# Third group of x transposed by DMA, three groups' scales made at once, GpSimd's work reordered around the second group's gelu scale

## The chip, the cores and the metric

One core of one Trainium2 chip. The metric is the device time of one execution in microseconds (us). The kernel before takes 410.85 us, the median of three runs (410.72 to 411.11).

## What is computed

x has S = 2048 tokens of D = 448 channels, F is 1792.

```
xn = layernorm(x)
A  = irfft2(rfft2(xn) * (w_r + i w_i))
h  = gelu(layernorm(xn) @ w1)                 # [S, D]
hs = concat(shift(h[:, 0:112], +1), shift(h[:, 112:224], -1),
            shift(h[:, 224:336], +2), shift(h[:, 336:448], -2)) @ w2
x1 = xn + hs
h2 = gelu(layernorm(x1) @ w3) @ w4
out = x + A + x1 + h2
```

The shifts run along the tokens and fill with zeros. The change is in the part up to hs; what follows it on TensorE is w3, w4 and the Fourier filter.

## The kernel before

x lies in 16 blocks of 128 tokens, `xb(b)`, each [128, 448], two to a tile `xt`. They are worked on in four groups, GRP = [14, 15, 0, 1], [2, 3, 4, 5], [6, 7, 8, 9], [10, 11, 12, 13], called groups 0 to 3 below (the title's third group is group 2). Every float32 factor of a product is split into a float16 high part and the float16 remainder, and every product is three passes of float16 matmuls into PSUM. A row of 448 channels takes four slices of channels, the last of them 64 wide, which is why a 448 x 448 product of one block has 11 matmuls.

For each group the front part of the kernel does this:

- `norm1(g)`: statistics of each block on VectorE (L306, L307), a start value of 1/sqrt by integer arithmetic (L323 to L326), the negative mean (L328), and then each block is normalised in place with this start value (L333, L336) by the engine that `apply` names. The start value is exact enough for a float16 split once the later scales correct it.
- `refine()`, ten small operations on GpSimd (L345 to L354): the accurate 1/sqrt, and `gsc`, the scale under the first gelu.
- `scales()`, eight small operations on GpSimd (L358 to L365): `cs`, by which the block is scaled where hs is added, and the scale and bias of xn for the filter.
- The block is turned, so that channels lie on the partitions, and split. `T1(g)` with `transpose_split` does this for groups 0 to 2: TensorE transposes (L387, 16 for a group) into a PSUM bank, ScalarE copies the high part out (L391), VectorE subtracts (L401). `turn(3)` does it for group 3: ScalarE copies the high part (L868), VectorE makes the remainder in two pieces (L869, L870), and one DMA transpose per block on SyncE's queue (L871) writes the turned float16 block.
- `w1_unit(g, i)`: 11 matmuls (L427), gelu on ScalarE (L467), the high part on ScalarE (L468), the remainder in two halves on VectorE (L470). The pieces are written into a shifted layout in `x2mem`, and where a block of shifted h is complete, a DMA transpose turns it (L478).
- `w2_tile(b)`: 11 matmuls with the turned h block (L486) and an evacuation on VectorE that needs `cs` (L487).

Weights are scaled by a power of two from their mean square. `powers` makes it: squares on ScalarE (L253), a sum on VectorE (L258), a matmul with ones (L260), five small VectorE operations. `split_w` then splits: for w2 GpSimd scales (L276), ScalarE copies the high part (L277), GpSimd subtracts (L278); two DMAs copy parts of w2p to the other partitions (L933, L934). The last part of w3 and 1344 KB of w4 (`w3raw`, L223, and `w4half`, L238) are loaded behind the last h transpose of group 1.

The first units of group 0 are computed side by side in four PSUM banks, `first`. Units 22 and so on are unit 2 of group 2. A tile scheduler puts the instructions of each engine in one fixed order, and each engine and each DMA queue takes its own in that order. `behind(key)` says that what follows in the block is put after the instructions named; `pins` do that for the statistics of single blocks. SyncE's queue holds loads, h transposes and x transposes together. After the front part come tiles 4 to 7, units of group 3 (30 to 33), and, from the first L407 on, w3.

Of the kernel before, what the change touches and what calls it, by code (L numbers as in the profile page):

```python
# [32 lines left out]
EPS = 1e-5  # L33
# [3 lines left out]
PIN = [("a3",), ("a3",), ("a3",), ("a3",)]  # L37
# [88 lines left out]
def body(tc, nc, x, wf, w1, w2, w3, w4, c_g, c_n, c_small, out):  # L126
# [185 lines left out]
    xn_scale, xn_bias = {}, {}  # L312

    def norm1(g, apply, pins=None):

        bs = GRP[g]
        n, b0 = len(bs), bs[0]
        mv = pc.tile([128, 4, 2], F32, name=f"mva{b0}")
        stats([xb(b) for b in bs], f"a{b0}", mv, pins)
        a = pc.tile([128, 2 * n], F32, name=f"va{b0}")  # L320
        yi = pc.tile([128, 2 * n], I32, name=f"vy{b0}")
        y = yi.bitcast(F32)
        V.tensor_scalar(out=a[:, n:], in0=mv[:, :n, 1], scalar1=1.0 + EPS, scalar2=EPS * EPS, op0=ALU.mult, op1=ALU.add)  # L323
        V.tensor_scalar(out=a[:, 0:n], in0=mv[:, :n, 1], scalar1=EPS, scalar2=None, op0=ALU.add)
        V.tensor_single_scalar(yi, a.bitcast(I32), 1, op=ALU.logical_shift_right)
        V.tensor_scalar(out=yi, in0=yi, scalar1=-1, scalar2=0x5F3759DF, op0=ALU.mult, op1=ALU.add)  # L326
        nm = pc.tile([128, n], F32, name=f"nma{b0}")
        i = V.scalar_tensor_tensor(out=nm, in0=mv[:, :n, 0], scalar=-1.0, in1=y[:, n:], op0=ALU.mult, op1=ALU.mult)  # L328
        after["c", g] = (i.ins,)
        for k, b in enumerate(bs):  # L330
            y_, m_ = y[:, n + k:n + k + 1], nm[:, k:k + 1]
# [3 lines left out]
            else:  # L335
                i = apply[k].tensor_scalar(out=xb(b), in0=xb(b), scalar1=y_, scalar2=m_, op0=ALU.mult, op1=ALU.add)  # L336
                if apply[k] is V:
                    after["n", g] = (i.ins,)

        q, z = (pc.tile([128, 2 * n], F32, tag=f"v{t}", bufs=2, name=f"v{t}{b0}") for t in "qz")  # L340
        w, r = (pc.tile([128, 2 * n], F32, name=f"v{t}{b0}") for t in "wr")
        nm1 = pc.tile([128, n], F32, name=f"nm{b0}")

        def refine():
# [9 lines left out]
            P.tensor_scalar(out=gsc[:, 4 * g:4 * g + 4], in0=r[:, n:], scalar1=r1, scalar2=None, op0=ALU.mult)  # L354

        def scales():
            c, r1st, u = cs[:, 4 * g:4 * g + 4], w[:, 0:n], w[:, n:]
            P.tensor_tensor(out=r1st, in0=r[:, 0:n], in1=y[:, 0:n], op=ALU.mult)  # L358
            P.tensor_tensor(out=u, in0=r[:, n:], in1=r[:, n:], op=ALU.mult)
            P.tensor_tensor(out=c, in0=y[:, n:], in1=a[:, n:], op=ALU.mult)  # L360
            P.tensor_tensor(out=c, in0=c, in1=u, op=ALU.mult)
            P.tensor_tensor(out=c, in0=c, in1=r1st, op=ALU.mult)
            P.tensor_scalar(out=c, in0=c, scalar1=s12[:, 0:1], scalar2=None, op0=ALU.mult)
            P.tensor_tensor(out=nm1, in0=mv[:, :n, 0], in1=r1st, op=ALU.mult)
            P.tensor_scalar(out=nm1, in0=nm1, scalar1=-1.0, scalar2=None, op0=ALU.mult)  # L365
            for k, b in enumerate(bs):
                xn_scale[b], xn_bias[b] = r1st[:, k:k + 1], nm1[:, k:k + 1]
        return refine, scales
# [11 lines left out]
    def transpose_split(srcs, dst, key, ts=range(4), at=0, tags=("tr",) * 4, late=None):  # L380
        c = slice(128 * at, 128 * at + 128 * len(srcs))
        for t in ts:
# [9 lines left out]
            todo.append((key, t, i, lo, pt, dst[:w, t, c]))  # L392
        if late is None:
            low()

    todo = []

    def low():
        while todo:
            key, t, i, lo, pt, hi = todo.pop(0)  # L400
            j = V.tensor_tensor(out=lo, in0=pt, in1=hi, op=ALU.subtract)  # L401
            after[key, t] = after[key] = i.ins, j.ins
# [486 lines left out]
    with behind("e1"):  # L889
        low()  # L890
    for t in range(4):
        if t >= 1:
            with behind("p1"):
                T1(0, [t])
# [220 lines left out]
```

## Time and profile before

| what | us |
|---|---|
| median of three runs | 410.85 |
| profiled execution | 410.88 |
| its span | 409.1 |
| PE busy in the span | 400.4 (98%) |
| DVE, ACT, POOL busy | 336.9, 256.1, 103.2 |

PE, DVE, ACT, POOL and SP are TensorE, VectorE, ScalarE, GpSimd and SyncE. PEld is the weight load of a matmul, SPq the time that SyncE's queue takes to issue a DMA. A timeline row is the start, the duration of the stretch, the engine, the line, the operation, the tile written and the tiles read, the shape, and the count; what stands in brackets is the time that the engine idled just before, and what ended it. A row `xN` in a timeline gives N of them that follow each other. A DMA row in the list of issues is the size and the median time from issue to landing. The granted clock of TensorE is 1.00 at full rate.

### The profile page before, as it was taken

The page shows a single profiled execution, that of the slowest core. Times are in us where ns is not written, and L with a number is a line of the kernel's source. Part 1 is how long each engine was busy: PE and PEld are TensorE (multiplying, and loading weights), DVE is VectorE, ACT ScalarE, POOL GpSimd, SP SyncE. Part 2 cuts the span into 40 slices and gives each one's busy share as a digit, 9 for nine tenths or more (in the row PEclk, how much of TensorE's full clock was granted, in tenths as well). Part 3 has the DMA queues.
Part 4 walks back from the last instruction along what each step waited for, and adds up shares of the span by engine and source line. Part 5 has one row for each costly group of instructions (what it writes and reads, how often), then busy time and mean ns, then how long its engine had stood idle before and what let it go on. Part 6 is the DMA issues. An engine that isn't in the chain of part 4 may idle for free.

```text
span 409.1 us, 8749 instructions
## 1 busy us (share of the span) xinstructions
PE 400.4 (98%) x3391; PEld 297.5 (73%) x3391; DVE 336.9 (82%) x702; ACT 256.1 (63%) x434; POOL 103.2 (25%) x173
## 2 busy tenths in 40 slices
PE   8899999999999999999999999999999999999996
PEld 3455545765667777877787887877777779998995
DVE  5998999999856895998798888956899999965645
ACT  4689699882558866655598878863454445453431
POOL 7787630112145948310022111110000000000000
PEclk9999999999999999999999999999999999999999
DMA  8977995558779652536255666510011023100101
GB/s 275 373 286 139 238 177 140 110 115 178 102 200 292 219 151 77 182 136 179 68 144 143 155 149 164 146 31 13 22 70 69 24 85 96 46 2 2 45 2 45
DMA packets 54596, 52.07 MB, mean 127 GB/s; under 512 B 35678, under 2 KB 48542, under 8 KB 54556
## 3 DMA queue, kind: packets, MB, share of 16 engines
q1 hardware_dynamic: 54556, 51.53, 46.4%
q8 instruction: 26, 0.43, 0.4%
q14 instruction: 14, 0.11, 0.1%
HBM read 38.28 MB, written 3.67 MB: 103 GB/s over the span
## 4 chain that ended last, share of the span: by engine, by line
PE 86%; DVE 5%; DMA 3%; POOL 2%; ACT 1%; SPq 1%; issue 1%
PE pw L407 33%; PE acc L816 23%; PE pw L486 6%; PE side L786 4%; PE acc L786 3%; PE pu L675 3%; PE ps L575 3%; PE pe L696 2%; PE pp L630 2%; PE px L647 2%; PE py L717 2%; PE pw L427 2%; DMA xt<-x 1%; DVE sta L306 1%; DVE xT L401 1%; DMA w2p<-w2p 1%
## 5 line engine op out<-in xcount | busy, mean ns | idle before, releaser
L407 PE MATMUL pw<-x2mem,w3p 128*128 128x256 f16 x1232 | 152.0, 273 | 0.0
L407 PEld LDWEIGHTS <-w3p 128*128 128x128 f16 x1232 | 119.0, 98 | 19.6
L816 PE MATMUL acc<-w4p,hf 128*128 128x448 f16 (+1 forms) x516 | 104.2, 348 | 0.0
L816 PEld LDWEIGHTS <-hf 128*128 128x128 f16 x516 | 50.1, 98 | 37.5
L734 ACT ACTIVATE pw<-pw,pe 128x512 f32<-128x512 f32 x42 | 27.5, 654 | 31.7 <-PE pw L407 31.6
L737 DVE SCALAR_TENSOR_TENSOR hf<-pw,h,hf 128x512 f16<-128x512 f32 x42 | 31.3, 745 | 12.7 <-ACT hf L736 12.4
L486 PE MATMUL pw<-w2p,h 128*128 128x448 f16 x176 | 35.7, 353 | 1.6 <-DMA h<-x2mem 1.2
L427 PE MATMUL pw<-w1p,xT 128*128 128x448 f16 x176 | 34.8, 352 | 0.7 <-ACT w1p L280 0.4
L656 POOL TENSOR_TENSOR z<-te 128x450 f32<-128x450 f32 x16 | 15.7, 981 | 70.7 <-DVE te L654 65.8
L736 ACT ACTIVATE hf<-pw,h 128x512 f16<-128x512 f32 x42 | 28.8, 685 | 5.0 <-PE acc L816 4.0
L486 PEld LDWEIGHTS <-h 128*128 128x128 f16 x176 | 17.1, 98 | 17.2 <-DMA h<-x2mem 1.9
L427 PEld LDWEIGHTS <-xT 128*128 128x128 f16 x176 | 17.2, 98 | 16.6 <-issue 1.1
L752 ACT ACTIVATE hz<-g,h 128x896 f16<-128x896 f32 x14 | 14.6, 1042 | 22.9 <-DVE g L749 22.9
L786 PEld LDWEIGHTS <-hz 128*128 128x128 f16 x294 | 28.2, 98 | 0.6
L637 ACT ACTIVATE pf<-pp 64x450 f16<-64x450 f32 x32 | 17.3, 542 | 12.6 <-DVE pf L638 9.6
L638 DVE TENSOR_TENSOR pf<-pp,pf 64x450 f16<-64x450 f32 x32 | 19.9, 622 | 5.1 <-ACT pf L637 4.8
L753 DVE SCALAR_TENSOR_TENSOR hz<-g,h,hz 128x896 f16<-128x896 f32 x14 | 16.1, 1147 | 6.7 <-ACT hz L752 6.7
L558 POOL TENSOR_TENSOR f<-xr 128x452 f32<-128x452 f32 x16 | 19.7, 1250 | 0.6
L566 DVE TENSOR_TENSOR xh<-f,xh 128x452 f16<-128x452 f32 x16 | 14.3, 916 | 4.9 <-ACT xh L565 4.9
L652 ACT ACTIVATE te<-px 64x450 f32<-64x450 f32 x32 | 17.3, 540 | 1.2 <-PE px L647 0.6
L746 ACT ACTIVATE g<-pw,pe 128x512 f32<-128x512 f32 x14 | 9.6, 683 | 11.4 <-PE pw L407 11.4
L555 POOL TENSOR_TENSOR xr<-xf 128x452 f32<-128x452 f32 x8 | 9.2, 1154 | 24.4 <-issue 17.6
(188 smaller groups left out, 712.5 us busy)
## 6 DMA issues: line engine op xcount, KB each, us to landing
wc<-wf SPq DMA_DIRECT2D x32, 225.0 KB, 3.7
wl<-wf SPq DMA_DIRECT2D x8, 450.0 KB, 4.2
xt<-x SPq DMA_DIRECT2D x8, 448.0 KB, 7.8
xf<-x SPq DMA_DIRECT2D x8, 448.0 KB, 4.9
loads<-x SPq DMA_DIRECT2D x7, 448.0 KB, 3.5
out<-xt SPq DMA_DIRECT2D x13, 224.0 KB, 1.9
w3raw<-w SPq DMA_DIRECT2D x3, 896.0 KB, 11.3
gn<-c_g SPq DMA_DIRECT2D x16, 128.0 KB, 3.1
```

Of the source, the lines that this page charges most:

```text
L407: T.matmul(ps_out, wp[:, wi + t, cols], xT[:, xi + t, tok], start=t == 0 and wi + xi == 0, stop=t == 3 and wi == 4)
L427: T.matmul(pm[:, :D], xTs[g][:, xi + t, 128 * i:128 * i + 128], w1p[:, wi + t], start=t == 0 and p == 0, stop=t == 3 and p == 2)
L486: T.matmul(pm[:, :D], h[:, k], w2p[:, w], start=n == 0, stop=n == 10)
L558: P.tensor_tensor(out=f[:, :, k:k + 2].rearrange("p b s d -> p s b d"), in0=u[:, :, 0], in1=u[:, :, 1], op=op)
L637: A.activation(out=hi, in_=src, func=AF.Copy)
L638: V.tensor_tensor(out=lo, in0=src, in1=hi, op=ALU.subtract)
L652: A.activation(out=e[64 * h:64 * h + 64], in_=px_[64 - 64 * h:128 - 64 * h, :2 * DF], func=AF.Copy)
L734: A.activation(out=pm, in_=pm, func=AF.Gelu_apprx_tanh, scale=r3)
L736: i = A.activation(out=h[:, 0], in_=pm, func=AF.Copy, scale=h3)
L737: j = V.scalar_tensor_tensor(out=h[:, 1], in0=pm, scalar=h3, in1=h[:, 0], op0=ALU.mult, op1=ALU.subtract)
L786: m = T.matmul(to, h[:, hi, 128 * blk:128 * blk + 128], b[wi], start=new and n == 0, stop=n == 2 and (last if blk in (2, 5, 3, 0) else end ...
L816: m = T.matmul(to, h[:, hi, o:o + 128], w4p[0][:, wi, f, r], start=first and f % 2 == 0 and n == 0, stop=end and f % 2 == 1 and n == 2, sk ...
```

## The change

`turn` takes the side of its staging tile and the engines for the remainders, and is called for group 2, `turn(2, 0, (V, V, V, V))`, in place of `T1(2)`. Sixteen TensorE transposes, four copies (L391) and four subtractions (L401) go; four copies (L860), eight subtractions (L862, L863) and four DMA transposes (L864) come.

`scales` is a function of its own, and the tiles that it reads (`mva`, `va`, `vw`, `vr`, `vy`) hold all 16 blocks. It is called once for groups 0 to 2, behind the refinement of group 2, and once for group 3: 16 operations, before 32.

The rest is order: all four slices of group 0 are transposed behind w1's power matmul; units 0 and 1 of group 0 are finished ahead of group 1's transposes, units 2 and 3 behind w2's power matmul, which itself comes behind unit 1; block 0 is normalised on GpSimd and not on ScalarE; w2 is split behind group 1's gelu scale on GpSimd and not behind a normalisation of group 2 on ScalarE; the two memsets of the wrap move behind group 2's gelu scale; pins differ.

```diff
-PIN = [("a3",), ("a3",), ("a3",), ("a3",)]
+PIN = [("b0",), ("b0",), ("b0",), ("b0",)]
...
+            i = P.tensor_scalar(out=gsc[:, c], in0=r[:, 1], scalar1=r1, scalar2=None, op0=ALU.mult)
+            after["g", g] = (i.ins,)
+        return refine
+
+    def scales(g, n):
+
+        o = slice(4 * g, 4 * g + 4 * n)
+        c, r1st, u, y, r = cs[:, o], vw[:, 0, o], vw[:, 1, o], vy[:, :, o], vr[:, :, o]
+        P.tensor_tensor(out=r1st, in0=r[:, 0], in1=y[:, 0], op=ALU.mult)
...
+        P.tensor_scalar(out=c, in0=c, scalar1=s12[:, 0:1], scalar2=None, op0=ALU.mult)
+        P.tensor_tensor(out=nm1[:, o], in0=mva[:, o, 0], in1=r1st, op=ALU.mult)
+        P.tensor_scalar(out=nm1[:, o], in0=nm1[:, o], scalar1=-1.0, scalar2=None, op0=ALU.mult)
...
     def wrap_on():
         move(pairs[1], pairs[0], -1)
-        P.memset(pairs[0][0:1], 0.0)
-        P.memset(pairs[2], 0.0)
...
-    def turn(g):
+    def turn(g, side=1, engines=(V, V, V, V)):
 
         xTs[g] = p1.tile([128, 7, 512], F16, tag="xT", bufs=2, name=f"xT{g}")
-        y = stage(f"x{g}", 8 * D, 1, F16).rearrange("p (i n) -> p i n", i=4)
+        y = stage(f"x{g}", 8 * D, side, F16).rearrange("p (i n) -> p i n", i=4)
         for i, b in enumerate(GRP[g]):
             h, x_ = y[:, i], xb(b)
             u = A.activation(out=h[:, 0:D], in_=x_, func=AF.Copy)
-            V.tensor_tensor(out=h[:, 448:512], in0=x_[:, 384:448], in1=h[:, 384:448], op=ALU.subtract)
-            v = V.tensor_tensor(out=h[:, 512:896], in0=x_[:, 0:384], in1=h[:, 0:384], op=ALU.subtract)
+            e = engines[i]
+            e.tensor_tensor(out=h[:, 448:512], in0=x_[:, 384:448], in1=h[:, 384:448], op=ALU.subtract)
+            v = e.tensor_tensor(out=h[:, 512:896], in0=x_[:, 0:384], in1=h[:, 0:384], op=ALU.subtract)
             d = SY.dma_start_transpose(out=xTs[g][:, :, 128 * i:128 * i + 128], in_=h)
...
-    n1 = [norm1(0, [P, V, A, V])]
-    T1(0, range(1), True)
+    n1 = [norm1(0, [P,V,P,V])]
...
-    n = 1
+    n = 2
     for unit in list(enumerate(first))[:n]:
         w1_in(0, [unit], [2, 3])
...
-    n1.append(norm1(1, [P, V, A, V], [("n", 0), ("r1",), ("a0", 0), ("a0", 1)]))
+    n1.append(norm1(1, [P, V, A, V], [("r1",), ("a0", 0), ("w1", 0), ("w1", 1)]))
...
-    with behind("n", 1):
+    with behind("n", 1), behind("u"):
         s2, r2 = powers(m2, 1, "2", first[0][:, 448:512])
+    with behind("p2"):
+        for unit in list(enumerate(first))[2:]:
+            w1_in(0, [unit], [2, 3])
...
-    with behind("a1"):
-        n1.append(norm1(2, [P, V, A, P]))
+    with contextlib.nullcontext():
+        n1.append(norm1(2, [P, V, A, P], [("n", 1), ("n", 1), ("e2",), ("e2",)]))
...
-    with behind("na", 2):
+    with behind("g", 1):
         for k in range(4):
             r = slice(0, 128 if k < 3 else 64)
-            split_w(w2p[r, k], w2p[r, 7 + k], w2s[r, k], s2[r], P)
+            after["w2", k] = split_w(w2p[r, k], w2p[r, 7 + k], w2s[r, k], s2[r], P)
         SY.dma_start(w2p[64:128, 3:7], w2p[0:64, 0:4])
         SY.dma_start(w2p[0:64, 4:7], w2p[64:128, 0:3])
     for k in range(4):
         w1_unit(1, k)
-    T1(2)
+    turn(2, 0, (V, V, V, V))
     with behind("h", 1, 3):
         load_w3([3])
         load_w4(8, 6)
-    n1[2][0]()
-    for n in n1:
-        n[1]()
+    n1[2]()
+    with behind("g", 2):
+        P.memset(pairs[0][0:1], 0.0)
+        P.memset(pairs[2], 0.0)
+    scales(0, 3)
```

The order on the engines differs in the front part only. SyncE's queue, before: h blocks of group 0 and 1's units (`h_470`), then the loads of `w3raw` and `w4half`, then blocks of the next h tile and of group 3's x.

```order
L933 DMA w2p<-w2p 64x1792
L934 DMA w2p<-w2p 64x1344
L478 DMA_TRANSPOSE h_470<-x2mem 128x7x128 x3
L223 DMA w3raw<-w 64x1792 x2
L238 DMA w4half<-w 128x6x448
L478 DMA_TRANSPOSE h_635<-x2mem 128x7x128
L871 DMA_TRANSPOSE xT_757<-x_758 128x7x128 x2
```

SyncE's queue in the change, from the copies of w2p to the same place (`xT_507` is group 2's x, `xT_709` group 3's):

```order
L925 DMA w2p<-w2p 64x1792
L470 DMA_TRANSPOSE h_454<-x2mem 128x7x128
L864 DMA_TRANSPOSE xT_507<-x_508 128x7x128 x2
L470 DMA_TRANSPOSE h_454<-x2mem 128x7x128 x2
L864 DMA_TRANSPOSE xT_507<-x_508 128x7x128 x2
L470 DMA_TRANSPOSE h_454<-x2mem 128x7x128
L223 DMA w3raw<-w 64x1792 x2
L238 DMA w4half<-w 128x6x448
L864 DMA_TRANSPOSE xT_709<-x_710 128x7x128 x2
L470 DMA_TRANSPOSE h_587<-x2mem 128x7x128
```

Four x transposes now stand among the four h transposes ahead of the loads, the w2p copies stand ahead of the first h transpose, and the first transpose behind the loads is one of group 3's x.

TensorE, before, at the end of group 1's units (`pw_13` is unit 3 of group 1, `pta` a bank of transposed slices, `pw_0` tile 0):

```order
L427 MATMUL pw_13_506<-w1p,xT_324 128x448
L387 MATMUL pta_524<-ident,xt_79 128x128 x2
L387 MATMUL pta_524<-ident,xt_80 128x128 x2
L387 MATMUL pta_530<-ident,xt_79 128x128 x2
L387 MATMUL pta_530<-ident,xt_80 128x128 x2
L387 MATMUL pta_536<-ident,xt_79 128x128 x2
L387 MATMUL pta_536<-ident,xt_80 128x128 x2
L486 LDWEIGHTS h_470
L486 MATMUL pw_0_705<-w2p,h_470 128x448
```

TensorE in the change, where the matmuls of one unit or tile (11 of each, each with its weight load) are shown by one row of each kind:

```order
L420 LDWEIGHTS xT_322
L420 MATMUL pw_13_490<-w1p,xT_322 128x448
...
L478 LDWEIGHTS h_454
L478 MATMUL pw_0_657<-w2p,h_454 128x448
...
L420 MATMUL pw_22_606<-w1p,xT_507 128x448
```

Tile 0 now follows group 1's last unit with nothing between, and unit 22, the first of group 2, follows tile 0.

GpSimd, before, around group 2's normalisation (`vy_412`, `nma_417` and `xt_79`, `xt_80` are group 2's):

```order
L451 MEMSET x2mem 1x1792
L345 TENSOR_TENSOR vq_423<-vy_412 128x8
L360 TENSOR_TENSOR cs<-vy_412,va_411 128x4
L336 TENSOR_SCALAR xt_79<-xt_79,vy_412,nma_417 128x448
L336 TENSOR_SCALAR xt_80<-xt_80,vy_412,nma_417 128x448
L346 TENSOR_TENSOR vq_423<-vq_423,va_411 128x8
L278 TENSOR_TENSOR w2p<-w2s,w2p 128x448
```

GpSimd in the change, at the same place:

```order
L352 TENSOR_SCALAR gsc<-vr,pe_205 128x4
L276 TENSOR_SCALAR w2s<-w2s,pe_355 128x448 x3
L276 TENSOR_SCALAR w2s<-w2s,pe_355 64x448
L278 TENSOR_TENSOR w2p<-w2s,w2p 128x448 x3
L343 TENSOR_TENSOR vq_412<-vy 128x8
L362 TENSOR_TENSOR cs<-vy,va 128x12
L336 TENSOR_SCALAR xt_79<-xt_79,vy,nma 128x448
L336 TENSOR_SCALAR xt_80<-xt_80,vy,nma 128x448
L278 TENSOR_TENSOR w2p<-w2s,w2p 64x448
```

Three of w2's four subtractions now stand ahead of group 2's normalisation, directly behind the scalings; before they stood behind it, and a memset stood ahead.

More of the change, by code (lines that the diff above doesn't have):

```diff
@@ L854, in body, with T1 @@
     flat = lambda t: t.rearrange("p a n -> p (a n)")
-    def T1(g, ts=range(4), late=None):
+    def T1(g, ts=range(4)):
         if g not in xTs:
@@ L959, in body @@
     turn(3)
-    n1[0][0]()
-    n1[0][1]()
+    n1[0]()
+    scales(3, 1)
     ln2([0, 1], [A, P])
```

88 lines of the change are left out of this document (35 added, 53 removed).

## The prediction

> **What bounds the kernel now.** I read the page's chain of work first, then the busy time of each engine in windows, then the timelines of TensorE, SyncE, VectorE and GpSimd over 14 to 80 us. The chain, and the windows (start:end and length, busy us of PE, PEld, DVE, ACT and POOL, granted clock, DMA share, GB/s):
>
> ```profile
> PE 86%; DVE 5%; DMA 3%; POOL 2%; ACT 1%; SPq 1%; issue 1%
> ```
>
> ```profile
> 30.00:40.00 10.00, 9.05 (x55) 5.32 (x54) 8.39 (x20) 9.97 (x18) 8.69 (x22) 1.00 0.69 132
> 50.00:60.00 10.00, 9.21 (x49) 4.55 (x48) 9.71 (x34) 9.97 (x20) 4.33 (x13) 1.00 0.87 168
> 120.00:409.00 289.00, 285.81 (x2720) 230.84 (x2718) 232.40 (x407) 167.07 (x285) 52.75 (x50) 1.00 0.34 99
> ```
>
> TensorE sets the end. It idles under 1 us in 30 to 40 and in 50 to 60, and 3.2 of 289 us from 120 on. The two kernels issue the same instructions in the same order on PE from the first L400 (L407 before) on, so the change is worth as much as it moves that point. Here is what PE does until then (start, us, tile, count, idle before it and who ended it):
>
> ```profile
> 19.34 0.38 PE L260 MATMUL pw<-pt,ones 128*128 128x1 f32 x2 [0.75 <-DVE pt L258]
> 20.18 1.97 PE L387 MATMUL pta<-ident,xt 128*128 128x128 f32 x16 [0.46 <-POOL xt L336]
> 21.98 11.32 PE L427 MATMUL pw<-w1p,xT 128*128 128x448 f16 x59
> 33.15 1.47 PE L387 MATMUL pta<-ident,xt 128*128 128x128 f32 x12
> 35.12 1.31 PE L486 MATMUL pw<-w2p,h 128*128 128x448 f16 x6 [0.51 <-DMA h<-x2mem]
> 36.27 0.60 PE L387 MATMUL pta<-ident,xt 128*64 128x128 f32 x4
> 37.69 0.73 PE L486 MATMUL pw<-w2p,h 128*128 128x448 f16 x3 [0.45 <-DMA w2p<-w2p]
> 55.43 2.24 PE L427 MATMUL pw<-w1p,xT 128*128 128x448 f16 x11
> ```
>
> ```profile
> 70.84 0.60 PE L407 MATMUL pw<-x2mem,w3p 128*128 128x256 f16 x4
> ```
>
> One matmul of 448 columns is paced at 11.32/59, about 0.19 us; the landmark is 70.84. The profiled execution took 410.88 us, 0.03 over the median; its span is 409.1, so 1.8 us lie around it.
>
> **What the change takes from TensorE.** The 16 transposes of the third group cost 1.47 + 0.60 = 2.07 us, and the waits of 0.51 and 0.45 stand among them. The copies of w2p (0.45) are issued earlier and should be in place. At the front, group 1's transposes waited 0.75 + 0.46 us. GpSimd's normalisation ended that wait, and it stood behind small scale operations that now come later:
>
> ```profile
> 19.42 0.71 POOL L336 TENSOR_SCALAR xt<-xt,vy,nma 128x448 f32<-128x448 f32 x1
> ```
>
> It can start about 1 us sooner, at the end of the gelu scale; and unit 1 of group 0 (5 matmuls, 0.95 us) now fills the idle time. I put the transposes at 19.2 instead of 20.18, with unit 1 done ahead of them. Group 1's last matmul then ends near 33.15 − 1.0 − 0.8 = 31.4 (0.8 taken of the 0.95, as the fit is not perfect). That is 1.8 us won. By then PE is through with 1.8 + 2.07 us that the old kernel still had ahead.
>
> **What it waits for next: the first h block.** Tile 0 is now next on PE, with nothing in front of it to fill the time. It needs the first h transpose (here from issue, SPq) and its landing:
>
> ```profile
> 32.09 1.34 SPq L478 DMA_TRANSPOSE h<-x2mem  x1
> 34.80 4.37 SPq L478 DMA_TRANSPOSE h<-x2mem  x3
> 39.23 1.22 SPq L223 DMA_DIRECT2D w3raw<-w  x2
> 40.49 0.59 SPq L238 DMA_DIRECT2D w4half<-w  x1
> 46.16 1.23 SPq L478 DMA_TRANSPOSE h<-x2mem  x1
> ```
>
> It was issued at 32.09, tile 0 began at 35.12: about 3.03 us later. The issue comes from a VectorE chain that the change lengthens in front: w2's power matmul now stands behind unit 1 and group 1's transposes, so its scale, made at 20.3, comes later. These are the scale's last step, the subtractions of transposed slices and the block statistics on VectorE, and the w2 scalings on GpSimd:
>
> ```profile
> 20.21 0.14 DVE L267 TENSOR_SCALAR pe<-pe 128x1 int32<-128x1 int32 x1
> 22.83 1.99 DVE L401 TENSOR_TENSOR xT<-pta,xT 128x512 f16<-128x512 f32 x3
> 24.86 2.21 DVE L306 BATCH_NORM_STATS2 sta<-xt 128x6 f32<-128x448 f32 x4
> ```
>
> ```profile
> 21.28 1.26 POOL L276 TENSOR_SCALAR w2s<-w2s,pe 128x448 f32<-128x448 f32 x2
> ```
>
> Four subtractions of 0.66 us now stand ahead of the scale on VectorE, from about 20.5 (0.8 behind the first transposes): with two statistics and the scale's own five steps between them I estimate it at 24.1. GpSimd's four scalings of 0.63 us follow, to 26.6, then its first three subtractions (L278, 1.0 us each) to 29.8. VectorE, with two more statistics (0.55 each) and unit 0's remainder (0.8) behind the scale, reaches group 2's small operations (L324 to L328) at the same moment, about 26.6. What such company does is in these rows:
>
> ```profile
> 16.79 1.03 DVE L325 TENSOR_SCALAR vy<-va 128x8 int32<-128x8 int32 x1
> 28.09 1.01 DVE L323 TENSOR_SCALAR va<-mva 128x4 f32<-128x4 f32 x1
> 29.35 0.17 DVE L326 TENSOR_SCALAR vy<-vy 128x8 int32<-128x8 int32 x1
> 29.76 0.51 DVE L336 TENSOR_SCALAR xt<-xt,vy,nma 128x448 f32<-128x448 f32 x1
> 30.19 2.24 DVE L470 SCALAR_TENSOR_TENSOR x2mem<-pw,h,x2mem 128x224 f16<-128x224 f32 x6
> ```
>
> ```profile
> 16.76 1.03 POOL L278 TENSOR_TENSOR w1p<-w1s,w1p 128x448 f16<-128x448 f32 x1
> 27.49 1.58 POOL L451 MEMSET x2mem<- 1x1792 f16 x1
> 32.90 3.01 POOL L278 TENSOR_TENSOR w2p<-w2s,w2p 128x448 f16<-128x448 f32 x3
> ```
>
> The same 8-column operation took 0.17 us alone and 1.03 us when it began 0.03 us after a GpSimd subtraction of 1.03 us: it lasted until that one ended. The memset at 27.49 held one for 1.01 in the old order; it is gone from this place, three subtractions of 1.0 us each stand there instead.
>
> [...]
>
> From the normalisation's start (29.76) to the first h issue (32.09) are 2.33 us: the normalisation, then half-block remainders of three units. Without company, five small operations of 0.2 us each from 26.6 put it at 27.6 + 2.33 = 29.95; with each held to a subtraction's end, at 29.8 + 0.8 + 2.33 = 32.9. I take 31.8, nearer to the late end, since the operations come one after the other into three subtractions that stand back to back, and a free gap between them is short. Tile 0 starts at 31.8 + 3.05 = 34.85. **So TensorE idles from about 31.4 to 34.85, and nearly all that was won is waited away.**
>
> **The queue behind it.** SyncE issues in order. Before, four h transposes stood ahead of the loads of w3raw and w4half; now eight transposes do. The three after the first lasted 4.37 us with their data waits; a transpose alone takes 1.25 to 1.34 of the queue (1.34 at 32.09, 1.23 at 46.16), 1.29 taken. So the last of the eight is issued 7 × 1.29 = 9.0 after the first, at 40.8. Before, it was at about 37.9 (34.80 + 4.37 − 1.3). ScalarE gives about the same: two squares of w3raw (1.7 us each) now stand ahead of unit 3's copy, which then ends near 40.
>
> ```profile
> 37.40 1.68 ACT L253 ACTIVATE xr<-w3raw 128x1792 f16<-128x1792 f32 x1
> ```
>
> Then the loads follow, and behind them on PE's path, first of all, the transposes of group 3 (before: an h transpose, issued at 46.16). What that one waited for (its time to landing, and the usual one):
>
> ```profile
> DMA to landing us min/median/max: 5.6/5.6/5.6
> ```
>
> ```profile
> w4half<-w SPq DMA_DIRECT2D x1, 1344.0 KB, 10.5
> h<-x2mem SPq DMA_TRANSPOSE x9, 3.1
> ```
>
> Though issued 5.7 us after the w4half load, the transpose landed at 51.76, 0.77 us behind that load (40.49 + 10.5 = 50.99), not after 3.1 us. It queued behind the load's bytes. From the last h issue to that landing it was 51.76 − 37.9 = 13.8 us. In the new order group 3's first transpose stands in that position, and unit 30 needs it: it lands at 40.8 + 13.8 = **54.6**. On its own work PE would reach unit 30 earlier: 34.85 plus 8 tiles' and units' worth of 11 matmuls each up to there (tiles 0 to 3, units 22, 20, 21, 23: 88 × 0.19 = 16.7) is 51.6, and 0.5 to 1.5 for waits on single blocks makes 52 to 53. PE waits there for some 2 us more.
>
> **The sum.** From unit 30 to L400 are 88 matmuls (units 30 to 33, tiles 4 to 7), 16.65 us, and 0.2 for changes between them: 54.6 + 16.65 + 0.2 = 71.45, or 71.5 against 70.84, +0.64. Other edits I take at nothing: scales made at once come at about 45, and the first evacuation that would hold a bank is needed at 47 to 48 (cover 2 us; if it is gone, the excess adds to tile 2); the memsets and moved pins fall in time that GpSimd has (4.33 us busy of 10 in 50 to 60; without it, they would add their 1.6 us to the scales). ACT and VectorE copies and subtractions of a block replace those of a transposed slice one for one. Forecast 410.88 + 0.64 = 411.5 us. In short: the difference is the first h issue less 31.16, where 31.16 is the issue at which the loads' chain would meet 70.84.
>
> **Rivals.**
>
> *The gain stays.* If VectorE finds GpSimd's gaps, h is issued at 29.95 to 30.5 and everything on the queue follows: 29.95 − 31.16 = −1.2, 409.7 us. The old loads also ended thinly, by the last column of these windows (GB/s):
>
> ```profile
> 43.85:48.65 4.80, 4.80 (x27) 2.45 (x25) 4.50 (x17) 4.24 (x7) 4.16 (x9) 1.00 1.01 309
> 48.65:50.45 1.80, 1.80 (x11) 0.96 (x10) 1.45 (x5) 1.80 (x5) 1.43 (x5) 1.00 1.55 122
> ```
>
> The tail's 1.8 us at 122 GB/s would be 0.7 us at 309. Without all of it but 0.4 the transposes land 1.4 us sooner: −2.6, 408.3 us. For it: the old order won when a memset went by. Against: the subtractions stand there by the order, not by chance.
>
> *Slower: VectorE is held by all three subtractions.* Then h is issued at 32.9, +1.75, 412.6 us. It decides from 31.98 on (31.16 + 0.82). Place: L324 to L328 within 26.6 to 29.8. For it: the two rows of 1.03 and 1.01. Against: 0.17 at 29.35, when GpSimd had nothing long.
>
> *The idle time costs the clock.* PE would idle for 3.4 us. These rows show the clock falling after the last matmul (start, us; then the window's granted clock), and a slow start:
>
> ```profile
> 401.08 4.73 PE L816 MATMUL acc<-w4p,hf 128*128 128x448 f16 x36
> ```
>
> ```profile
> 408.00:409.00 1.00, 0.00 (x0) 0.00 (x0) 0.00 (x0) 0.00 (x0) 0.00 (x0) 0.74 0.00 0
> ```
>
> ```profile
> 5.80 2.90 PEld L846 LDWEIGHTS <-wsrc 128*128 128x128 f16 x14 [0.20 <-issue]
> ```
>
> PE's last matmul ends at 405.81, and the mean clock of 0.74 in 408 to 409 means half rate from about 408.5: 2.7 us after. At the start, the weights went 0.21 us apart (2.90/14) only after 5.80 us, 4.6 us into the warm-up. A fall here would double 2.2 us' worth of matmuls, +2.2 us on tiles 0 and 22; but the wait for group 3's transpose swallows 1.6 to 2 of it. It adds about 0.6, 412.1 us. [...]
>
> *The change does not pay because it was hidden anyway.* Group 3's transpose lands no later than needed, and the 2.07 us are waited at tile 0: 410.9 ± 0.5.
>
> **How the numbers follow.** A measurement of this kernel tells about 0.2%, 0.82 us, from no change. Forecast (with the hidden case): 0.44, of which some falls outside 0.82. The gain stays: 0.24. VectorE held by all three: 0.20. The clock falls: 0.12. Faster by over 0.82: 0.22; within: 0.38; slower: 0.40. Range: from 409.0 (most of the gain case) to 413.0 (both slower cases, with 0.4 for their overlap). Likeliest 411.5.
>
> **What would show it.** Group 1's transposes at about 19.2 and its last matmul near 31.4; first h issue at 31.8; PE idle before tile 0 about 3.4 us, released by the DMA of h; VectorE's L324 to L328 with one or more of 1.0 us; the w3raw loads at about 42; unit 30 released by the DMA of xT at 54.6; L400 at 71.5; granted clock 1.00 in 30 to 40. I'd be wrong if unit 30 follows its predecessor without idle time (then the loads don't bind), or if VectorE's small operations all take 0.2 us.

## The result, and the profile after

| | us, median | range | ratio to the kernel before, 95% |
|---|---|---|---|
| before, same chip | 410.98 | 410.72 to 411.59 | |
| changed | 414.84 | 414.11 to 415.01 | 1.0088, 1.0071 to 1.0106 |

The change costs 3.9 us. The profiled execution took 415.01 us, 4.13 over the one before, and its span is 413.2. The forecast was 411.5, its range ended at 413.0. The direction "slower" had a chance of 0.40, and the size lies outside the range.

The chain of waits and the windows at the places shown of before (the same columns). TensorE's share of the chain fell from 86 to 81%, and DMA's rose from 3 to 6%:

```profile
PE 81%; DVE 7%; DMA 6%; ACT 2%; SPq 2%; issue 1%; ACTq 0%; DVEq 0%
```

```profile
30.00:40.00 10.00, 5.61 (x21) 2.31 (x20) 9.82 (x34) 9.13 (x16) 8.70 (x17) 0.70 0.55 107
50.00:60.00 10.00, 8.58 (x47) 4.60 (x46) 8.90 (x42) 7.67 (x15) 1.52 (x5) 1.00 1.10 250
```

Where PE was busy 9.05 of 10 us from 30 to 40, it is busy 5.61, at a mean clock of 0.70. PE's timeline shows the two waits in this part:

```profile
19.53 1.96 PE L389 MATMUL pta<-ident,xt 128*128 128x128 f32 x16 [0.65 <-POOL xt L336]
21.47 10.38 PE L420 MATMUL pw<-w1p,xT 128*128 128x448 f16 x54
36.24 4.29 PE L478 MATMUL pw<-w2p,h 128*128 128x448 f16 x11 [4.39 <-DMA h<-x2mem]
40.32 2.46 PE L420 MATMUL pw<-w1p,xT 128*128 128x448 f16 x11
56.80 2.25 PE L420 MATMUL pw<-w1p,xT 128*128 128x448 f16 x11 [1.42 <-DMA xT<-x]
73.46 1.04 PE L400 MATMUL pw<-x2mem,w3p 128*128 128x256 f16 x8
405.81 4.17 PE L808 MATMUL acc<-w4p,hf 128*128 128x448 f16 x33
```

Up to the end of group 1's units, at 21.47 + 10.38 = 31.85, the change wins nearly what was expected (31.4 was forecast). Then PE stands still for 4.39 us, and its first 11 matmuls behind that take 4.29 us for a work of 2.24. Unit 30, at 56.80, waits again. The last matmul ends at 409.98, before at 405.81: 4.17 later. Taken between the same matmuls of both kernels, 2.8 of it are there at 109 us and 4.1 from 121 on.

Why the first h block is late, on VectorE and on GpSimd:

```profile
26.80 3.36 DVE L324 TENSOR_SCALAR va<-mva 128x4 f32<-128x4 f32 x1
30.07 0.16 DVE L325 TENSOR_SCALAR va<-mva 128x4 f32<-128x4 f32 x1
```

```profile
27.11 3.02 POOL L278 TENSOR_TENSOR w2p<-w2s,w2p 128x448 f16<-128x448 f32 x3
```

One operation of 4 columns lasts 3.36 us. It ends at 30.16, GpSimd's three subtractions at 30.13; the same kind of operation behind it takes 0.16. VectorE found no gap between the subtractions at all.

SyncE's queue behind it, and the landing of its x transposes:

```profile
33.20 1.34 SPq L470 DMA_TRANSPOSE h<-x2mem  x1
34.73 2.57 SPq L864 DMA_TRANSPOSE xT<-x  x2
37.39 2.59 SPq L470 DMA_TRANSPOSE h<-x2mem  x2
40.04 2.63 SPq L864 DMA_TRANSPOSE xT<-x  x2
42.76 1.25 SPq L470 DMA_TRANSPOSE h<-x2mem  x1
44.07 1.22 SPq L223 DMA_DIRECT2D w3raw<-w  x2
46.09 8.57 SPq L864 DMA_TRANSPOSE xT<-x  x2
```

```profile
DMA to landing us min/median/max: 2.6/3.0/10.7
```

The eight transposes go one after the other, 9.56 us from the first issue to the last. The loads of w3raw stand at 44.07, before at 39.23. The two x transposes behind the loads take 8.57 us to issue instead of 2.57, and the worst one lands 10.7 us after its issue.

The granted clock, in three stretches of 3.41 us (start:end, length, then busy us of PE, PEld, DVE, ACT and POOL; the clock is third from the end):

```profile
30.51:33.92 3.41, 1.34 (x8) 0.49 (x5) 3.34 (x11) 3.05 (x6) 3.11 (x7) 1.00 0.04 11
33.92:37.33 3.41, 1.09 (x3) 0.43 (x4) 3.41 (x11) 3.41 (x6) 2.79 (x8) 0.50 0.72 136
37.33:40.75 3.42, 3.42 (x11) 1.41 (x10) 3.38 (x11) 3.19 (x6) 3.42 (x4) 0.50 0.94 178
```

TensorE's clock is halved for 6.8 us. Of that, 2.3 us fall on idle time (33.92 to 36.24); tile 0 and the start of unit 22 run in the other 4.5 and pay 2.05 and 0.22 us.

Far behind all this, at 119.5 us, a third wait appears, and ScalarE shows where it is from:

```profile
119.49 0.55 PE L808 MATMUL acc<-w4p,hf 128*128 128x448 f16 x2 [0.72 <-ACT hf L728]
120.28 2.06 PE L808 MATMUL acc<-w4p,hf 128*128 128x448 f16 x10 [0.24 <-DVE hf L729]
```

```profile
115.30 0.67 ACT L499 ACTIVATE y<-xt,nm 128x448 f32<-128x448 f32 x1 [3.20 <-DMA x2mem<-y]
117.50 0.67 ACT L499 ACTIVATE y<-xt,nm 128x448 f32<-128x448 f32 x1 [1.53 <-DMA x2mem<-y]
118.07 0.64 ACT L726 ACTIVATE pw<-pw,pe 128x512 f32<-128x512 f32 x1
```

A gelu (L726) stands behind two normalisations (L499) that wait for a transfer of y. In the kernel before, the order on ScalarE at this place was gelu (L734), normalisation, normalisation (L507):

```profile
109.05 0.66 ACT L734 ACTIVATE pw<-pw,pe 128x512 f32<-128x512 f32 x1 [1.82 <-PE pw L407]
110.15 0.67 ACT L507 ACTIVATE y<-xt,nm 128x448 f32<-128x448 f32 x1 [0.44 <-DMA x2mem<-y]
112.21 0.67 ACT L507 ACTIVATE y<-xt,nm 128x448 f32<-128x448 f32 x1 [1.38 <-DMA x2mem<-y]
```

The second normalisation also comes 5.3 us later than before (117.50 against 112.21), TensorE at this place only 2.8. So the orders of the two kernels differ not only in the front part. ScalarE's still differs here, and TensorE's is not the same from the first L400 on either: the same matmuls of w2, w3 and w4 follow, but in other groups (the kernel before issues 4 of w3, 11 of w2 and 60 of w3, the changed one 8, 11 and 51), and the order is the same only from 104 us in the kernel before and 107 us in the change. TensorE does not wait in that stretch in either kernel: it is 2.6 us behind at its start and 2.8 at its end.

### The profile page after: what moved, and what is told of

It is laid out like the page before. It is cut to its first block, busy times and chain, and to the rows that moved or that the text cites. A ratio compares the mean times of both kernels' runs of the same rounds, so it can differ in the third digit from the quotient of the medians.

```text
span 413.2 us, 8719 instructions
## 1 busy us (share of the span) xinstructions
PE 401.1 (97%) x3375; PEld 296.2 (72%) x3375; DVE 337.1 (82%) x706; ACT 255.4 (62%) x433; POOL 102.2 (25%) x158
## 4 chain that ended last, share of the span: by engine, by line
PE 81%; DVE 7%; DMA 6%; ACT 2%; SPq 2%; issue 1%; ACTq 0%; DVEq 0%
PE pw L400 31%; PE acc L808 20%; PE pw L478 6%; PE side L778 4%; PE acc L778 3%; PE pw L420 3%; PE pu L667 3%; PE ps L567 3%; DMA xT<-x 3%; PE pe L688 2%; PE pp L622 2%; PE px L639 2%; PE py L709 2%; DMA xt<-x 2%; DMA x2mem<-y 1%; DVE xT L394 1%
## 5 line engine op out<-in xcount | busy, mean ns | idle before, releaser
L400 PE MATMUL pw<-x2mem,w3p 128*128 128x256 f16 x1232 | 152.2, 273 | 0.0
L400 PEld LDWEIGHTS <-w3p 128*128 128x128 f16 x1232 | 119.0, 98 | 20.0
L726 ACT ACTIVATE pw<-pw,pe 128x512 f32<-128x512 f32 x42 | 27.4, 654 | 28.6 <-PE pw L400 28.3
L729 DVE SCALAR_TENSOR_TENSOR hf<-pw,h,hf 128x512 f16<-128x512 f32 x42 | 31.3, 746 | 15.3 <-ACT hf L728 15.0
L478 PE MATMUL pw<-w2p,h 128*128 128x448 f16 x176 | 37.6, 367 | 4.4 <-DMA h<-x2mem 4.4
L420 PE MATMUL pw<-w1p,xT 128*128 128x448 f16 x176 | 35.2, 354 | 1.6 <-DMA xT<-x 1.4
L478 PEld LDWEIGHTS <-h 128*128 128x128 f16 x176 | 17.6, 101 | 21.1 <-DMA h<-x2mem 5.1
L420 PEld LDWEIGHTS <-xT 128*128 128x128 f16 x176 | 17.2, 99 | 18.1 <-DMA xT<-x 1.5
L738 ACT ACTIVATE g<-pw,pe 128x512 f32<-128x512 f32 x14 | 9.6, 685 | 11.4 <-PE pw L400 11.4
L462 DVE SCALAR_TENSOR_TENSOR x2mem<-pw,h,x2mem 128x224 f16<-128x224 f32 x32 | 12.5, 441 | 4.9 <-ACT x2mem L460 4.9
```

What stands on the lines that cost most here:

```text
L400: T.matmul(ps_out, wp[:, wi + t, cols], xT[:, xi + t, tok], start=t == 0 and wi + xi == 0, stop=t == 3 and wi == 4)
L420: m = T.matmul(pm[:, :D], xTs[g][:, xi + t, 128 * i:128 * i + 128], w1p[:, wi + t], start=t == 0 and p == 0, stop=t == 3 and p == 2)
L478: T.matmul(pm[:, :D], h[:, k], w2p[:, w], start=n == 0, stop=n == 10)
L726: A.activation(out=pm, in_=pm, func=AF.Gelu_apprx_tanh, scale=r3)
L729: j = V.scalar_tensor_tensor(out=h[:, 1], in0=pm, scalar=h3, in1=h[:, 0], op0=ALU.mult, op1=ALU.subtract)
```

## Experiments

**Theory A**: the whole loss comes from the first h issue. VectorE is held by the three subtractions, h is late, and the eight transposes push the loads and group 3's transposes back by as much. **Theory B**: PE's idle time costs the clock, and that is what reaches the end. **A third theory**: the swap itself costs, by four more transposes on SyncE's queue ahead of the loads, however early the first is. Most kernels keep the changed kernel's order on every engine and queue by a table of numbers, and move only the rows named. In those all lines stand 90 further down (L568 is tile 0's L478, L510 a unit's L420, L560 an h transpose L470, L954 an x transpose L864, L414 is L324, L368 is L278, L490 is L400). Times are medians; the ratio is against the kernel before on the same chip, which took 410.79 to 410.99 us in the three groups of runs.

### The changed kernel again

> The changed kernel itself with its orders kept by a table and nothing moved: 414.8, as measured (414.11 to 415.01), first h issue at 33.2. It is the measure for the runs that keep the orders.

Unchanged but for the table. It took 415.03 us, 1.0098 (1.0083 to 1.0112). The median repeats, but not the way there: in this execution no wait of 0.7 us stands at 119.5, and the clock fell twice, for 3.41 us each, and 20.48 us lie between the two starts:

```profile
33.38:36.79 3.41, 0.61 (x4) 0.34 (x5) 3.41 (x12) 3.41 (x7) 2.75 (x9) 1.00 0.64 123
36.79:40.20 3.41, 3.41 (x11) 1.38 (x10) 3.38 (x13) 3.41 (x6) 3.36 (x3) 0.50 0.87 163
53.86:57.27 3.41, 1.48 (x10) 0.88 (x8) 3.41 (x22) 2.60 (x6) 0.26 (x1) 1.00 1.29 167
57.27:60.68 3.41, 3.41 (x12) 1.37 (x9) 1.03 (x9) 0.13 (x1) 0.19 (x1) 0.50 0.85 189
```

In the 3.41 us ahead of the two falls PE worked for 0.61 and 1.48 us. The wait for group 3's transpose (1.93 us) is all of PE's idle time in the second of these.

### The three subtractions behind the normalisation

```diff
 GpSimd's order
-L278 TENSOR_TENSOR w2p<-w2s,w2p 128x448 x3
 L343, L362, L336, L336 (group 2)
+L278 TENSOR_TENSOR w2p<-w2s,w2p 128x448 x3
 L278 TENSOR_TENSOR w2p<-w2s,w2p 64x448
```

> The changed kernel with every engine's order kept, but for one thing: GpSimd's three subtractions of w2 (L278) stand behind its two normalisations of group 2 instead of ahead of them. Theory A (one VectorE operation is held until the three subtractions end, 3.36 us, and the first h block, the queue and TensorE's waits follow): VectorE's small operations of group 2 take 0.2 us each, the first h transpose is issued near 30.0 instead of 33.20, tile 0 starts near 33.1 instead of 36.24, the granted clock stays 1.00 in 30 to 40, unit 30 starts near 53.6 instead of 56.80; 411.6 us, and 410.5 if the later wait for the gelu goes too. Rival B (VectorE waits there for something else, such as the w2 scale): nothing moves, 414.8. Rival C (group 3's x transposes are late by their own data): the first h block comes early, unit 30 stays within 1 us of 56.8, 414 to 415.

It took 413.79 us, 1.0069 (1.0057 to 1.0081): 1.05 less than the change. VectorE's timeline (L414, and L953, the remainder of an x block, which comes once more at 32.44), then GpSimd's, the queue's and PE's:

```profile
26.26 0.37 DVE L414 TENSOR_SCALAR va<-mva 128x4 f32<-128x4 f32 x1
30.14 1.40 DVE L953 TENSOR_TENSOR x<-xt,x 128x384 f16<-128x384 f32 x1
```

```profile
29.10 4.32 POOL L368 TENSOR_TENSOR w2p<-w2s,w2p 128x448 f16<-128x448 f32 x4
```

```profile
29.67 1.34 SPq L560 DMA_TRANSPOSE h<-x2mem  x1
```

```profile
32.72 2.25 PE L568 MATMUL pw<-w2p,h 128*128 128x448 f16 x11 [1.40 <-ACT x L950]
36.94 2.25 PE L510 MATMUL pw<-w1p,xT 128*128 128x448 f16 x11 [1.97 <-DMA xT<-x]
55.31 3.94 PE L510 MATMUL pw<-w1p,xT 128*128 128x448 f16 x11 [1.79 <-DMA xT<-x]
```

The operation is down from 3.36 to 0.37 us, and the first h is issued 3.5 us sooner; 0.5 of this is the front of this execution (group 1's transposes at 19.00, in the change 19.53). So the hold was the cause of the late issue. But tile 0 and unit 22 start 3.5 and 3.4 sooner, unit 30 only 1.5. The subtractions now hold the remainders of group 2's x (1.40 where the change had 0.57 us), and the last of the eight transposes is issued at 41.11, 1.65 sooner. At unit 30 the clock fell, as in the repeat. Theory A is right in the mechanism and wrong in the size.

### One subtraction ahead instead of three

```diff
 GpSimd's order
 L278 TENSOR_TENSOR w2p<-w2s,w2p 128x448
-L278 TENSOR_TENSOR w2p<-w2s,w2p 128x448 x2
 L343, L362, L336, L336 (group 2)
+L278 TENSOR_TENSOR w2p<-w2s,w2p 128x448 x2
```

> The changed kernel with its orders kept, and of GpSimd's three subtractions of w2 one ahead of its normalisations of group 2 and two behind. If VectorE's operation is held for as long as GpSimd's subtractions follow each other: the operation at the start of group 2's small ones takes up to 1.3 us (3.36 with three ahead, 0.37 with none), the first h issue comes between e1's 29.67 and 31, tile 0 between 32.7 and 34; the time as e1's, 413.8, since VectorE's x remainders are held instead. If the length is set by something else, 3 us or more are waited again and h is issued at 33.

It took 413.65 us, 1.0062 (1.0050 to 1.0075). The operation's row:

```profile
26.81 1.37 DVE L414 TENSOR_SCALAR va<-mva 128x4 f32<-128x4 f32 x1
```

With none, one and three subtractions ahead it lasts 0.37, 1.37 and 3.36 us: one subtraction's length more for each. (With none it ends at 26.63, with GpSimd's scalings at 26.60.) The first h issue follows: 29.67, 31.23, 33.20. The last of the eight transposes hardly does (41.11, 41.55, 42.76), where the subtractions hold the x remainders instead, and the total does not: 413.79, 413.65, 414.84.

### The load of w4 early

```diff
     with behind("h", 1, 3):
         load_w3([3])
-        load_w4(8, 6)
+    load_w4(8, 6)
```

> The changed kernel with every engine's order kept, but for one thing: the 1344 KB load of w4half stands behind the first part of that load, near 15 us, instead of ahead of group 3's x transposes. Theory A (group 3's first x transpose waits behind the load's bytes): it is issued near 45.5 and lands by 50 instead of 56.8, unit 30 follows the power matmul at 55.4 without a wait, the two transposes of 4.39 and 4.07 us on SyncE's queue take 1.3 each; 413.4 us. Rival B (the data of group 3 or the transposes' own number sets it): unit 30 still waits until 56.8, 414.8. Rival C (the load in its new place slows the front's DMAs): the first h issue or its landing moves later than 33.20 and 36.24, 415 or more.

The 1344 KB are issued at 15.3 us. It took 412.28 us, 1.0037 (1.0023 to 1.0050), 2.6 less than the change, more than expected. The queue and PE:

```profile
45.52 2.72 SPq L954 DMA_TRANSPOSE xT<-x  x2
```

```profile
36.50 3.94 PE L568 MATMUL pw<-w2p,h 128*128 128x448 f16 x11 [4.69 <-DVE x2mem L552]
54.99 2.24 PE L510 MATMUL pw<-w1p,xT 128*128 128x448 f16 x11
```

Group 3's two transposes are issued in 2.72 us instead of 8.57, and unit 30 waits for nothing, though tile 0 waits as long as ever and the clock fell there. So it is the load's bytes that made unit 30 wait. The first wait alone still leaves the kernel slower than before.

### Both moves

```diff
-        load_w4(8, 6)
+    load_w4(8, 6)
...
 GpSimd's order
-L278 TENSOR_TENSOR w2p<-w2s,w2p 128x448 x3
 L343, L362, L336, L336 (group 2)
+L278 TENSOR_TENSOR w2p<-w2s,w2p 128x448 x3
```

> The changed kernel with the orders kept, and the moves of e1 and e2 together: GpSimd's three subtractions of w2 behind its normalisations of group 2, and the 1344 KB load of w4half near 15 us. If the late first h block and the load's bytes are the two causes: first h issue at 29.7 (e1 had 29.67), no wait of unit 30 for group 3's transpose, granted clock 1.00 from 30 to 60, the first L400 at 70 to 71 instead of 73.46; about 411.0, that is 1.3 below e2's 412.28 and level with the kernel before. Rival (ScalarE's and VectorE's own work sets the middle of the front, so that an earlier h block only moves the waits): within 0.5 of e2, 411.8 to 412.8.

It took 412.68 us, 1.0046 (1.0031 to 1.0062): not better than the early load alone. PE, and the h transposes' landing:

```profile
36.52 3.68 PE L568 MATMUL pw<-w2p,h 128*128 128x448 f16 x11 [4.69 <-DMA h<-x2mem]
```

```profile
DMA to landing us min/median/max: 2.9/3.0/6.3
```

The first h is issued at 30.17, but lands 6.3 us later. The early load, issued at 15.2, took 17.7 us to its landing, to 32.9. I read from this that the transpose fell in behind the load's bytes, as group 3's had done: one collision was traded for another. In the kernel with the early load alone, h is issued at 33.15, when the load is through (15.3 + 17.9 = 33.2); tile 0 starts 3.35 us behind that issue, at 36.50, 0.3 later than in the repeat.

### The idle time filled

```diff
+    fill = bank("mm", "fill")
+    extra = set()
+    with behind("u"):
+        for i in range(16):
+            m = T.matmul(fill, wsrc[:, 0:128], wsrc, start=True, stop=True)
+            extra.add(m.ins.name)
+    after["fill"] = (m.ins,)
...
-    for b in range(4):
+    with behind("fill"):
+        w2_tile(0)
+    for b in range(1, 4):
...
-    keep_order(tc, nc, ())
+    keep_order(tc, nc, extra)
```

Sixteen matmuls that nobody reads are put into the idle time ahead of tile 0; `extra` leaves them out of the table of orders.

> The changed kernel with every engine's order kept, and 16 matmuls of 512 columns without use (0.21 us each, 3.4 us) put between group 1's last unit and tile 0, where TensorE idled 4.39 us. Theory A (the idle time halves the clock, but the 2.05 us that tile 0 loses by it are hidden by the later wait for group 3's transpose): granted clock 1.00 in 30 to 50, tile 0 takes 2.24 us instead of 4.29, unit 30 still starts at 56.8 and waits 3.5 us instead of 1.42; 414.8 us. Rival B (the clock's fall costs the kernel its 2.05 us): unit 30 starts near 54.8, 412.8 us.

It took 413.94 us, 1.0068 (1.0055 to 1.0081). PE (L1023 is the filling):

```profile
31.65 3.62 PE L1023 MATMUL fill<-wsrc 128*128 128x512 f16 x16
36.20 2.25 PE L568 MATMUL pw<-w2p,h 128*128 128x448 f16 x11 [0.94 <-DMA h<-x2mem]
55.95 2.25 PE L510 MATMUL pw<-w1p,xT 128*128 128x448 f16 x11 [1.86 <-DMA xT<-x]
```

The clock was 1.00 throughout in this execution, which took 412.70, and no wait stood at 119.5. Three runs at a mean clock of 0.999 or 1.000 took 412.70, 413.04 and 413.68 us; three at 0.995 or 0.996 took 414.19, 414.51 and 414.52. So B holds for part of the loss, and the wait at unit 30 (1.86) for part, since it is still there. What a fall costs is not the same everywhere: with one subtraction ahead the two runs at 1.00 took 412.61 and 413.02 and the others 413.65 to 414.26, but with the late subtractions the one run at 1.00 took 413.79, no less than the other four (413.39 to 414.07). With the filling on top of the early load, where unit 30 does not wait either:

```diff
...
+            m = T.matmul(fill, wsrc[:, 0:128], wsrc, start=True, stop=True)
...
-        load_w4(8, 6)
+    load_w4(8, 6)
...
```

> The changed kernel with the orders kept, the load of w4half near 15 us as in e2, and the 16 matmuls of 512 columns without use in TensorE's idle time as in e4. If the fall of the clock costs its 2.05 us wherever no later wait swallows it: clock 1.00 throughout, tile 0 2.25 us, unit 30 near 53.0 instead of e2's 54.99, the first L400 at 69.6 instead of 71.63; 410.2, and the spread of e2's runs (411.61 to 413.89) shrinks to that of the kernel before, about 0.8. Rival (the lost 2 us come back on VectorE, which is busy without a gap from 60 to 80): 411.5.

It took 410.64 us, 0.9998 (0.9989 to 1.0006), 1.64 less than the early load alone, at a clock of 1.00. Unit 30:

```profile
54.29 2.24 PE L510 MATMUL pw<-w1p,xT 128*128 128x448 f16 x11
```

All of the change's loss is gone when neither the load's bytes nor the clock strike. The time that the filling and the rest of the wait take ahead of tile 0 is then about what the change had won on TensorE: the first matmul of w3 comes at 70.93, before at 70.84.

### The gelu first

```diff
 ScalarE's order at 115 to 119 us
-L499 x2, L726, L728
+L726, L499 x2, L728
```

> The changed kernel with every engine's order kept, but for one thing: on ScalarE the gelu of pw_05 (L726) stands ahead of the two subtractions of the mean for blocks 12 to 15 (L499), as it did in the kernel before. Theory A (the gelu stood in a queue behind two operations that waited for a DMA of their staging tile, and TensorE waited for it): TensorE's idle time of 0.72 and 0.24 us at 119.5 is gone, and the last matmul comes 1.0 us sooner: 413.8 us. Rival B (ScalarE and VectorE are late there for other reasons, from the front): the waits stay, 414.8.

It took 414.26 us, 1.0075 (1.0058 to 1.0091). Three runs took 413.0 to 413.5, three 415.0 to 415.2, so the median decides nothing. The profile is of a run of 415.0: the wait at 119.5 is gone from it, but the clock fell a second time at unit 30, which took 3.94 us. In the repeat, with such a fall and without the edit, the wait was gone as well. So this profile does not show that the edit removes the wait, and whether it changes the time of the kernel stays open.

### The transposes of group 2 back on TensorE

```diff
-    turn(2, 0, (V, V, V, V))
+    T1(2)
```

> The changed kernel with group 2 turned by T1(2) on TensorE, as in the kernel before, and all else as changed; the scheduler makes the order. If the DMA transposes are what costs (an empty TensorE before tile 0, and four more transposes ahead of the loads): first h issue still near 33.2, but TensorE has 2.07 us of transposes ahead of tile 0, the clock stays 1.00, the loads are issued about 4 us sooner and unit 30 doesn't wait; 411.0 to 411.5. Rival (the late h block alone costs): 413.5 or more.

All else of the change's code stays; the orders are made anew by the scheduler. It took 409.76 us, 0.9988 (0.9975 to 1.0001): 5.1 less than the change by the medians, and 4.1 by the two ratios (0.0100 of 411), since seven of its runs took 409.2 to 409.9, at a mean clock of 0.999 or 1.000, and five 411.1 to 411.9, at 0.994 or 0.995. Its lines are those of the changed kernel. The queue and PE:

```profile
32.95 5.36 SPq L470 DMA_TRANSPOSE h<-x2mem  x4
```

```profile
36.13 2.25 PE L478 MATMUL pw<-w2p,h 128*128 128x448 f16 x11 [1.07 <-DMA h<-x2mem]
55.01 2.24 PE L420 MATMUL pw<-w1p,xT 128*128 128x448 f16 x11
```

The first h is as late as in the change (32.95, VectorE is held for 3.35 us here too). But the 16 transposes stand where PE would idle, the four h transposes take 5.36 us of the queue instead of 10.81 for eight, the loads start at 38.37 instead of 44.07, unit 30 does not wait, and the clock stays at 1.00 in this execution. That is the third theory. The other way round, the kernel before with the DMA transposes alone:

```diff
-    def turn(g):
+    def turn(g, side=1):
...
-    T1(2)
+    turn(2, 0)
```

> The kernel before with group 2 turned by DMA (turn(2, 0)) and nothing else of the change; the scheduler makes the order, which puts the four x transposes directly ahead of the first h transpose. If the DMA transposes are what costs: first h issue pushed to 35 or so, TensorE idle for over 3 us before tile 0, the clock falls, group 3's x transposes land behind the loads at 56 or later; 413 to 414. Rival (the reordered GpSimd work costs, the transposes are free): 409 to 411.

It took 421.94 us, 1.0280 (1.0267 to 1.0294). The direction is that of the third theory, the size is far more than any theory gave. The scheduler ordered this kernel anew: four x transposes stand ahead of three of the h transposes (not of the first, as was expected), PE waits 3.6 us in all for h blocks and 3.13 for ScalarE at 80 us. The first matmul of w3 comes at 80.12, before at 70.84, so 9.3 of the 11 us are lost by then. They were not taken apart further, and since the scheduler changed more than the swap, this run does not price the swap.

### The two best together

```diff
 the kernel with T1(2), and in GpSimd's order
-L278 TENSOR_TENSOR w2p<-w2s,w2p 128x448 x3
 L343, L362, L336, L336 (group 2)
+L278 TENSOR_TENSOR w2p<-w2s,w2p 128x448 x3
```

> e7 (the changed kernel with group 2 turned on TensorE) with its orders kept, and GpSimd's three subtractions of w2 behind its normalisations of group 2, as in e1. If both causes are as told: VectorE's small operations take 0.2 us each, the first h issue comes at 29.8 instead of e7's 32.95, tile 0 follows the transposes without a wait near 33.6 instead of 36.13, clock 1.00, and no VectorE work is held instead, since its subtractions of transposed slices read PSUM; 407.5 to 408.5, below the kernel before. Rival (VectorE, busy without a gap later, takes the gain back): 409.5, as e7.

It took **407.11 us** (406.92 to 407.36), 0.9910 (0.9895 to 0.9925): 3.9 us less than the kernel before. PE, with the transposes of group 2 (L479):

```profile
31.42 1.91 PE L479 MATMUL pta<-ident,xt 128*128 128x128 f32 x16
33.16 2.24 PE L568 MATMUL pw<-w2p,h 128*128 128x448 f16 x11
52.03 2.24 PE L510 MATMUL pw<-w1p,xT 128*128 128x448 f16 x11
```

The 16 transposes fill the time that h needs to land, h is issued at 29.93, and PE waits for nothing at any of the three places. The three subtractions are all that differs from the kernel above with T1(2), on any engine or queue. Moving them is worth 2.65 us here by the medians, and 1.05 where eight transposes stand on the queue.

## Why the prediction was wrong

- *TensorE's front.* Group 1's transposes at 19.2, its last matmul at 31.4: measured 19.53 and 31.85. Right to half a microsecond; the 2.07 us of transposes and 1.3 at the front were won.
- *The chain of w2's scale.* Scale at 24.1, three subtractions from 26.6 to 29.8: measured 24.55, and 27.11 to 30.13. Right.
- *"I take 31.8"*, the first h issue. **This step failed.** Measured 33.20, later even than the late end of 32.9. The reason given, a free gap between the subtractions is short, but would be found, does not hold: none was found, one operation was held for all three, as the doses of 0.37, 1.37 and 3.36 us show. The rival with a chance of 0.20 had this mechanism, at 412.6 us. No rival reached the measured 414.84.
- *"The difference is the first h issue less 31.16"*. **This step failed too.** With the first h at 29.67 it gives 409.4 us, and the kernel took 413.79; at 31.23 it gives 410.95, and the kernel took 413.65. The loads wait for the last of the eight transposes, and that one does not follow the first by a fixed 9.0: it was issued at 41.11 and 41.55 there, 11.4 and 10.3 later, largely, as I read it, because VectorE was then held at the x remainders. The issue at 33.20 alone does not make the loss.
- *Landing* 3.05 after the issue: 3.04. *Queue* 9.0 from first to last issue: 9.56, since it took 1.37 and not 1.29 for a transpose. *Group 3's transpose behind the loads' bytes*, 13.8 after the last h issue: 14.04 (42.76 to 56.80). The mechanism is right, and the early load shows it. Unit 30 at 54.6 became 56.80: 1.40 from the issue, 0.56 from the queue, 0.24 from the landing.
- *From unit 30 to L400* 16.85: 16.66. L400 at 71.5 came at 73.46, 2.62 later than before. This is 2.6 of the 4.13 us.
- *"The wait for group 3's transpose swallows" the clock's fall.* In the profiled execution it did. In others a second fall follows the wait, at unit 30 (the repeat: 3.79 us for a work of 2.24), which nothing swallows. With the idle time filled the median is 0.9 us lower, the three runs without a fall are 1.8 lower (413.04 in the median), and where unit 30 does not wait the filling is worth 1.64.
- *Alike from L400 on.* **This failed as well**, in two ways. TensorE's order is not the same there, as shown above; 0.2 us more are lost over that stretch. And TensorE waits at 119.5, which cost 1.3 us in the profiled execution (2.8 to 4.1): the prediction names neither ScalarE nor the transfers of y there. The wait is there in the execution whose clock did not fall at unit 30, and not in the repeat, whose clock did: TensorE came to the matmuls at this place 1.4 us later in the repeat (117.74 against 116.34). What sets the time of the transfers of y stays open.
- *The sum*: +0.64 became 2.6 at L400 and 4.17 at the last matmul.
- *"Other edits I take at nothing"*: with the transposes back on TensorE the rest of the change is worth 0.5 us by its ratio, and the interval just reaches 1: right, as far as can be measured, but as a balance, since the order of the three subtractions alone costs 2.65 us of it. The loss is that of the swap: 2.07 us taken from TensorE, 4.1 to 5.1 lost by it.

## What to carry to other kernels

Work taken from the engine that bounds a kernel pays only if what stands behind it is ready: here the 16 transposes (1.91 us in the best kernel) filled the time in which a block had to land (3.0 us from its issue), and the queue that took them over (1.37 us for each of eight transposes) also carried the loads of the next stage. Where a small VectorE operation will stand beside a row of back-to-back GpSimd subtractions, measure its length for each number of them: L324 here lasted 0.37, 1.37 and 3.36 us with none, one and three. When orders of two kernels are called alike behind a point, compare them row by row, the bound engine's own and those of every engine that it waits for.

## What the runs showed of the hardware

- The clock of TensorE fell for stretches of 3.41 us. In seven traces taken apart from about 13 to 126 us (the change, its repeat, and the kernels with late subtractions, with one, with the early load, with both, with the gelu first), each fall lasted 3.41 us or twice that, at a clock of 0.50. In the two with two separate falls they began 20.48 us apart (at 36.79 and 57.27 in the repeat, at 36.42 and 56.90 with the gelu first). Laid out from a fall in steps of 3.41 us, the stretches just ahead of one at half rate had PE busy for 4, 6, 18, 19, 20, 32, 37, 39, 43 and 46% of the time. No stretch of 54% or more had a fall behind it, and there were also stretches of 40, 43 and 46% without one. One of these is from the kernel with both moves:

```profile
30.35:33.77 3.42, 1.47 (x8) 0.57 (x6) 3.42 (x5) 3.42 (x7) 3.42 (x4) 1.00 1.18 237
```

  So a share of 43 to 46% had a fall behind it in some executions and not in others. The same holds for a single wait of 1.8 to 1.9 us: 1.93 in the repeat and 1.85 with the gelu first had a fall behind them; 1.86 at the same place, with the idle time filled, had none. What decides between them these runs do not show.
- Behind the loads of w3raw and w4half, the issue of a DMA transpose on SyncE's queue lasted 4.39 and 4.07 us in the change (the two from 46.09 on), where the h transpose ahead of the loads took 1.25.
- Beside GpSimd's chain of w2's subtractions, some of VectorE's operations that read only SBUF lasted longer, and not all alike. The TENSOR_SCALAR of 4 columns lasted to the end of all three subtractions (3.36 us, 0.37 with none ahead). With the late subtractions, three TENSOR_TENSORs of the x remainders within the chain took 1.40, 1.05 and 1.40 us, where the change has 0.57, 0.21 and 0.55, and the four subtractions took 4.32 us, in the best kernel 4.01. Two operations that read PSUM took no longer: beside the same chain, from 29.36 to 33.37 in the best kernel, a subtraction of a transposed slice took 0.69 us (1.99 / 3 = 0.66 without it), and four half-block remainders (L552) took 1.52 us, 0.38 each (0.80 / 2 = 0.40 behind it).
